# mLSTM cell and mixture of depths on one core: gates of three chunks at once, a first step in its own order, a warm-up of TensorE, and the last batch's picks as matrix products

## Chip, cores, metric

The kernel runs on one core of one Trainium2 chip. The metric is the device time of one execution in microseconds (us).

## The reference

The first part is an mLSTM cell over 4 batches, 8 heads, 768 time steps and head size 40. The second is a mixture of depths: in each batch the 128 tokens with the highest score go through two dense layers (320 to 1024 to 320).

```python
for t in range(S):
    m_new = max(f[t] + m, i[t])
    C = exp(f[t] + m - m_new) * C + exp(i[t] - m_new) * outer(v[t], k[t])
    n = exp(f[t] + m - m_new) * n + exp(i[t] - m_new) * k[t]
    m = m_new
    y[t] = sigmoid(o[t]) * (C @ q[t]) / max(abs(n @ q[t]), 1)
x = y of all heads side by side              # (4, 768, 320)
scores = x @ w_gate
for b in range(4):
    top = the 128 tokens with the highest scores[b]
    out[b] = x[b]
    out[b, top] += sigmoid(scores[b, top]) * (relu(x[b, top] @ w1) @ w2)
```

## The kernel before, in words

The sequence is cut into chunks of 128 tokens, 6 per batch. A step n is one chunk c of one batch b, 24 steps in all. The order of instructions on every engine is that of the program; nothing reorders it.

**A step.** `step(n)` (L466) loads the chunk of step n+4 by four DMAs on SyncE's queue (k, q, v, output gate; `load_chunk`), which come in pieces of 160 bytes. `decay` (POOL, L279) scales the state C. `scores` does the products of keys and queries (PE, pS, L269) and multiplies them by the decay matrix W (DVE, P, L271). W for step n+2 is made in `weigh`: two products (pW, L249), exponential (ACT, L250), and the causal mask (POOL `affine_select`, L251). `scaled_v` makes wv (POOL, L259). `exchange` does the part that comes from the state (pIC, L291 and L297) and updates C. `within` does pH (PE, L319) from P. `norm` makes num, den, rec (DVE) and sor (POOL, L334). `turned(n+2)` turns the keys and queries of step n+2 (PE, pt, L229; ACT copies into T). `result` makes x (DVE, L339), stores it by SyncE, and makes the score sc (DVE, L342). One step later `spread` (PE pb, ACT) and `compare` (DVE ge, L355) count for each token how many score higher.

**The gates.** `gates(c0, c1)` (L162) does the prefix sums of one or two chunks on 32 partitions (4 batches by 8 heads), in three scans and an elementwise chain, and splits both results into three bfloat16 parts each. It is called in the prologue for chunks 0 and 1, and at the end of steps 0 and 2 for chunks 2, 3 and 4, 5. In batch 0, `first_weighed(n+2)` (L458) follows at the end of the step: `operands` (PE pO, ACT a_o, DVE M_o, L197), `weigh`, `scales` (ACT wk and r, L183), `columns` (PE pc, L206, DVE cols) and wv. From step 6 on, W and wv of step n+2 are made in the middle of step n, since the operands of all chunks exist; `operands(1, c)` for batches 2 and 3 are made in steps 4 to 9.

**The second stage.** For batch b-1 it is spread over the steps of batch b: in c=1 `columns_of`, `ranks` and the selection (sel, DVE, L375), in c=2 `gather` (token numbers pidx, then an indirect DMA xe by POOL, L386), in c=3 to 5 the first layer `first` (PE ph, L417, 2, 3 and 3 of 8 blocks f), and in c=0 and c=1 of the batch after it the second layer `second` (PE py, L426, 4 blocks f each), ye and the scatter by POOL (L431). The weights (2.56 MB) are loaded at the end of step 3. After step 23 comes a tail: the last score, comparison and ranks, `second` of batch 2, then for batch 3 the gather from HBM, turning (pX, L398), `first`, `second` and the scatter.

Of the kernel before, what the change touches and what calls it, by code (L numbers as in the profile page):

```python
# [27 lines left out]
def kernel(  # L28
# [123 lines left out]
    nM = gate.tile([BH, NT], FP, name="nM")
    wk = gate.tile([BH, NT, L], FP, name="wk")
    parts = [[gate.tile([BH, NT, L], BF, name=f"{x}{part}") for part in range(3)] for x in "Ma"]
    r = F
# [441 lines left out]
```

## Time and profile before

| | |
|---|---|
| median of 3 runs (lowest to highest) | 258.09 us (255.44 to 258.18) |
| profiled execution: its time, its span | 255.36 us, 253.6 us |
| PE, DVE, POOL, ACT busy | 191.0, 154.7, 104.5, 97.7 us |
| store of x issued, step 0, 5, 6, 12, 18 | 24.8, 94.5, 100.4, 142.6, 186.7 us |

The span is what the trace covers; the time is what is compared. A busy share is a mean over stages with different limits, so the run is read in four stages: until x of step 0, steps 1 to 5 (the rest of batch 0), steps 6 to 23, and the tail. Whenever a "granted clock" is given, 1.00 is 2.4 GHz and 0.50 is 1.2 GHz.

### The profile page before, as it was taken

The numbers are of one execution on the slowest core, as the hardware profiler recorded it, in microseconds if no ns is written. First come the engines' busy times: TensorE is split into PE (matmuls) and PEld (weight loads), VectorE is DVE, ScalarE is ACT, GpSimd is POOL, SyncE is SP. The second block draws the span as 40 slices with busy tenths as digits, with TensorE's granted clock in tenths as the row PEclk, the third lists the DMA queues.
The fourth block names the chain that finished last, engine by engine and source line by source line (L and its number), as shares of the span: only waits on it lengthen the run. The fifth ranks groups of instructions, "written<-read, shape, count | busy, mean of one in ns | idle before, by whom it ended". The sixth has DMA issues, their size and how long they took to land.

```text
span 253.6 us, 6331 instructions
## 1 busy us (share of the span) xinstructions
PE 191.0 (75%) x2522; PEld 160.6 (63%) x2522; DVE 154.7 (61%) x429; ACT 97.7 (39%) x218; POOL 104.5 (41%) x162
## 2 busy tenths in 40 slices
PE   1775366473576988977999999499999988780991
PEld 1464255362464866766999778499987878650880
DVE  7472625158173688889777666977766888740000
ACT  3633521504333565543556536155653641100010
POOL 5235452225316456573345637444563941102001
PEclk9995557575586899998899999889999999997598
DMA  8999900708008999778758987696986100001000
GB/s 111 163 145 145 143 0 16 116 1 125 8 0 270 248 157 145 127 129 141 115 90 127 142 125 98 124 134 103 128 141 83 54 28 27 30 24 52 3 0 27
DMA packets 105454, 24.37 MB, mean 96 GB/s; under 512 B 100496, under 2 KB 104784, under 8 KB 105424
## 3 DMA queue, kind: packets, MB, share of 16 engines
q1 hardware_dynamic: 104896, 22.47, 59.1%
q0 software_dynamic: 384, 1.31, 1.7%
q8 instruction: 20, 0.33, 0.6%
q10 hardware_dynamic: 144, 0.18, 0.3%
q14 instruction: 10, 0.08, 0.1%
HBM read 19.37 MB, written 4.59 MB: 94 GB/s over the span
## 4 chain that ended last, share of the span: by engine, by line
PE 35%; DVE 13%; issue 11%; POOL 5%; DMA 3%; POOLq 1%; ACT 0%; DVEq 0%
PE pH L319 9%; PE pS L269 5%; PE ph L417 5%; PE pt L229 4%; POOL sor L334 4%; PE py L426 3%; DVE x L339 3%; PE pIC L291 3%; DVE scr L342 2%; DVE P L271 2%; DMA out_dram<-ye,idx 2%; PE pIC L297 2%; PE pb L348 2%; DVE num L326 1%; PE pW L249 1%
## 5 line engine op out<-in xcount | busy, mean ns | idle before, releaser
L251 POOL TENSOR_SCALAR_AFFINE_SELECT W<-W 128x512 f32<-128x512 f32 x48 | 31.0, 669 | 54.4 <-ACT W L250 54.4
L334 POOL TENSOR_TENSOR sor<-so,rec 128x320 f32<-128x320 f32 x24 | 24.1, 1005 | 45.9 <-DVE rec L332 42.9
L319 PE MATMUL pH<-v,P 128*64 128x64 f32 x768 | 31.1, 235 | 12.2 <-DVE P L271 12.2
L229 PE MATMUL pt<-ident,qk 128*128 128x128 f32 x192 | 31.1, 314 | 11.7 <-POOL qk L105 6.4
L271 DVE TENSOR_TENSOR P<-pS,W 128x512 f32<-128x512 f32 x48 | 30.8, 682 | 10.4 <-PE pS L269 10.4
L319 PEld LDWEIGHTS pH<-v,P 128*64 128x64 f32 x768 | 27.6, 147 | 14.2 <-DVE P L271 13.4
L250 ACT ACTIVATE W<-pW 128x512 f32<-128x512 f32 x48 | 26.1, 595 | 26.8 <-PE pW L249 20.1
L230 ACT COPY T<-pt 128x512 f32<-128x512 f32 x48 | 26.5, 588 | 21.5 <-PE pt L229 21.5
L229 PEld LDWEIGHTS pt<-ident,qk 128*128 128x128 f32 x192 | 25.7, 162 | 12.7 <-POOL qk L105 6.9
L269 PE MATMUL pS<-T 64*128 64x128 f32 x384 | 32.5, 316 | 0.0
L269 PEld LDWEIGHTS pS<-T 64*128 64x128 f32 x384 | 27.4, 216 | 3.9 <-issue 2.1
L349 ACT COPY sb<-pb 128x128 f32<-128x128 f32 x24 | 6.4, 266 | 60.4 <-PE pb L348 60.4
L417 PE MATMUL ph<-xeT,w 128*128 128x128 f32 x192 | 27.0, 303 | 0.6 <-ACT xeT L400 0.6
L417 PEld LDWEIGHTS ph<-xeT,w 128*128 128x128 f32 x192 | 26.3, 221 | 1.0 <-ACT xeT L400 1.0
L339 DVE TENSOR_TENSOR x<-num,sor 128x320 f32<-128x320 f32 x20 | 14.0, 702 | 14.1 <-POOL sor L334 14.1
L426 PE MATMUL py<-w,hT 128*128 128x320 f32 x64 | 18.5, 434 | 0.0
L291 PE MATMUL pIC<-C,T 128*64 128x82 f32 x320 | 18.0, 262 | 0.0
L291 PEld LDWEIGHTS pIC<-C,T 128*64 128x64 f32 x320 | 14.5, 154 | 4.5 <-issue 3.4
L249 PE MATMUL pW<-M_o,a_o 32*128 32x512 bf16 x48 | 10.9, 427 | 8.4 <-DVE M_o L197 8.4
L431 POOL DMA_INDIRECT out_dram<-ye,idx x4 | 4.1, 1025 | 30.5 <-DVE ye L429 17.2
L355 DVE SCALAR_TENSOR_TENSOR ge<-sb,sc,earlier 128x128 bf16<-128x128 f32 (+5 forms) x24 | 15.7, 655 | 0.8 <-ACT sb L349 0.8
L259 POOL TENSOR_TENSOR wv<-v,cols 128x328 f32<-128x328 f32 x20 | 14.9, 743 | 3.1 <-DVE cols L208 2.4
(107 smaller groups left out, 270.9 us busy)
## 6 DMA issues: line engine op xcount, KB each, us to landing
qk<-in_k_dram SPq DMA_DIRECT2D x24, 160.0 KB, 3.4
qk<-in_q_dram SPq DMA_DIRECT2D x24, 160.0 KB, 4.2
v<-in_v_dram SPq DMA_DIRECT2D x24, 160.0 KB, 4.6
so<-in_o_gate_dram SPq DMA_DIRECT2D x24, 160.0 KB, 4.7
out_dram<-x SPq DMA_DIRECT2D x24, 160.0 KB, 1.8
w<-in_moe_w_dram SPq DMA_DIRECT2D x1, 1280.0 KB, 9.3
w<-in_moe_w_dram SPq DMA_DIRECT2D x2, 512.0 KB, 3.9
w<-in_moe_w_dram SPq DMA_DIRECT2D x1, 256.0 KB, 6.2
```

Of the source, the lines that this page charges most:

```text
L229: nc.tensor.transpose(pt[:, p, :], qk[:, j, 2 * p:2 * p + 2, :].rearrange("s a d -> s (a d)"), ident)
L230: nc.scalar.copy(out=T[:, j], in_=pt)
L250: nc.scalar.activation(out=W[:, h0:h0 + 4, :], in_=pW, func=AF.Exp)
L251: nc.gpsimd.affine_select(out=W[:, h0:h0 + 4, :], in_=W[:, h0:h0 + 4, :], compare_op=OP.is_ge, fill=0.0, base=0, pattern=[[0, 4], [1, L]], ...
L269: nc.tensor.matmul(pS[j][:, p, :], T[e, 0, p, :], T[e, 1, p, :], start=True, stop=True)
L271: nc.vector.tensor_tensor(out=P[:, :, j, :], in0=pS[j], op=OP.mult, in1=W.rearrange("p (n a) t -> p n a t", a=2)[:, :, j, :])
L291: nc.tensor.matmul(pI[t, 2 * p * D1:2 * (p + 1) * D1], T[:, 1, p, t], C[:, p].rearrange("e a d -> e (a d)"), start=True, stop=True)
L319: nc.tensor.matmul(pH[t, 2 * p + j, :], P[:, p, j, t], v1[:, 2 * p + j, :], start=True, stop=True)
L334: nc.gpsimd.tensor_tensor(out=sor, in0=so, in1=rec.unsqueeze(2).to_broadcast([128, H, D]), op=OP.mult)
L339: nc.vector.tensor_tensor(out=x.rearrange("p (h d) -> p h d", d=D), in0=num[:, :, 0:D], in1=sor, op=OP.mult)
L417: nc.tensor.matmul(self.ph[:, f % 4, :], w1[:, j, f * 128:(f + 1) * 128], self.xeT[:, j, :], start=(j == 0), stop=(j == NDC - 1))
L426: nc.tensor.matmul(self.py, self.hT[:, f, :], w2[:, f, :], start=(f == 0), stop=(f == NFC - 1))
```

## The change

- Three chunks lie side by side on 96 partitions (`NR`), so all 24 chunk-and-batch gates take two passes g. `scans` does the sums in each chunk from zero; `ends`, `carry` and `carried` bring the level m from chunk to chunk by small products on PE and one scan; `level` applies it; `split` makes the bfloat16 parts. Pass 0 and the operands of chunks 0 to 2 are done in the prologue, pass 1 beside step 0.
- `columns` turns three chunks at once. The gates come by six DMAs of 32 rows for each of f and i, three of them on SyncE ahead of the first chunk.
- The prologue loads five chunks; step 0 is written out by itself. `warm` runs 8 and then 1 products of 512 columns on a tile of ones that nothing reads.
- `step`: `weights(n+2)` in every step, `turned(n+2)` and `gated(n+2)` ahead of `within`; the causal mask and wv of step n+2 behind `norm`; `operands(0, n+3)` in steps 1 and 2, `operands(1, n-3)` in steps 3 to 8.
- `pieces` (new) deals out the second stage: the selection and gather at the end of steps c=1 and c=2, `first` in 3, 4 and 1 blocks and `second` in 3 and 5, with the scatter at the end of c=0. For batch 2 in the last batch: `first` 4 and 4, `second` 2 and 4, and 2 in the tail.
- Weights are loaded in five parts, one in each of steps 3 to 7.
- Tail: x of the last six steps stays in SBUF (six buffers). The picked rows, already turned, are products of x with the selection (float32, made in three parts): 18 products pX in place of the wait for the gather. The gather still runs, for the gate and the residual.

```diff
+    NR = 3 * BH
+    f_sb = [gate.tile([NR, L], FP, name=f"f_sb{g}") for g in range(2)]
...
+    def load_gates(eng, dst, src, g):
+        for c in range(3):
+            t = slice((3 * g + c) * L, (3 * g + c + 1) * L)
+            eng.dma_start(out=dst[g][c * BH:(c + 1) * BH], in_=src[:, :, t].rearrange("b h p -> (b h) p"))
...
+    def warm(n):
+        pw = ps_m.tile([128, 4 * L], FP, name="pw", tag="m")
+        for _ in range(n):
+            nc.tensor.matmul(pw, earlier[:, 0:128], earlier[:, 0:4 * L], start=True, stop=True)
+    def scans(g):
+        nc.vector.tensor_tensor_scan(out=FM[g][:, 0], data0=ones, data1=f_sb[g], initial=0.0, op0=OP.mult, op1=OP.add)
+        nc.vector.tensor_tensor(out=a[g], in0=i_sb[g], in1=FM[g][:, 0], op=OP.subtract)
+        nc.vector.tensor_tensor_scan(out=FM[g][:, 1], data0=ones, data1=a[g], initial=-BIG, op0=OP.mult, op1=OP.max)
+    def ends(g):
+        pe[g] = ps_m.tile([BH, 3, 2], FP, name="pe", tag="m")
+        for c in range(3):
+            nc.tensor.matmul(pe[g][:, c, :], ident[0:NR, c * BH:(c + 1) * BH], FM[g][:, :, L - 1], start=True, stop=True)
+    def carry(g):
+        e = gate.tile([BH, 3, 2], FP, name="e", bufs=2)
+        nc.vector.tensor_copy(out=e, in_=pe[g])
+        nc.vector.tensor_tensor_scan(out=m[:, 3 * g + 1:3 * g + 4], data0=e[:, :, 1], data1=e[:, :, 0],
+                                     initial=m[:, 3 * g:3 * g + 1], op0=OP.max, op1=OP.add)
+    def carried(g):
+        pm = ps_m.tile([NR, 3], FP, name="pm", tag="m")
+        for c in range(3):
+            nc.tensor.matmul(pm[c * BH:(c + 1) * BH], ident[0:BH, 0:BH], m[:, 3 * g:3 * g + 3], start=True, stop=True)
+        return pm
+    def level(g, pm):
+        own = gate.tile([NR, 3], FP, name="own", bufs=2)
+        nc.vector.tensor_tensor_reduce(out=own, in0=pm, in1=third, scale=1.0, scalar=0.0, op0=OP.mult, op1=OP.add,
+                                       accum_out=m_in[g])
+        nc.vector.tensor_scalar(out=FM[g][:, 1], in0=FM[g][:, 1], scalar1=m_in[g], scalar2=None, op0=OP.max)
+        nc.vector.tensor_scalar(out=nM[g], in0=FM[g][:, 1, L - 1:L], scalar1=-1.0, scalar2=None, op0=OP.mult)
+    def split(g, j, step, cast, sub):
+        x, xs = (FM[g][:, 1], a[g])[j], parts[j][g]
+        if step == 0:
+            rest[j] = gate.tile([NR, L], FP, name=f"rest{j}", bufs=2)
+            cast(out=xs[0], in_=x)
+            sub.tensor_tensor(out=rest[j], in0=x, in1=xs[0], op=OP.subtract)
+        else:
+            cast(out=xs[1], in_=rest[j])
+            sub.tensor_tensor(out=xs[2], in0=rest[j], in1=xs[1], op=OP.subtract)
...
+    def columns(g):
+        pc = ps_m.tile([128, 3, NR], FP, name="pc", tag="m")
+        for j, row in enumerate((wk[g], r[g], r[g][:, L - 1:L].to_broadcast([NR, L]))):
+            nc.tensor.transpose(pc[:, j, :], row, ident[0:NR, 0:NR])
+        both = const.tile([128, 3, NR], FP, name=f"cols{g}")
+        nc.vector.tensor_copy(out=both, in_=pc)
+        for c in range(3):
+            cols[3 * g + c] = both[:, :, c * BH:(c + 1) * BH]
...
+    def load_w1(j):
+        d0, w = HW[j]
...
+        return W
+    def causal(W):
+        for h0 in range(0, H, 4):
...
+        x = x_t[b, c] = work.tile([128, DM], FP, name="x", bufs=NT)
...
+    def select(sel, rank, t0, t1):
...
+    def pieces(b, c, when):
+        early = b == B - 1
+        if when == "late" and b > 1 and c == 0:
+            layers[b - 2].second(3, NFC)
+            layers[b - 2].leave()
+        if b == 0:
+            return
+        own = layers.get(b - 1)
+        if when == "rank":
+            if c == 1:
+                rank = ranks(columns_of(state[b - 1][1][2]), state[b - 1][1][3])
+                sel[b - 1] = mod.tile([128, NT, K_], HF, name="sel", bufs=1)
+                select(sel[b - 1], rank, 0, NT)
+            elif c == 2:
+                picked[b - 1] = gather(b - 1, sel[b - 1], token)
+        elif c == 3:
+            layers[b - 1] = own = Layers(b - 1, *picked[b - 1])
+            own.enter()
+            own.gate()
+            own.first(0, 4 if early else 3)
+        elif c == 4:
+            own.first(4 if early else 3, 8 if early else 7)
+            if early:
+                own.second(0, 2)
+        elif c == 5:
+            if early:
+                own.second(2, 6)
+            else:
+                own.first(7, 8)
+                own.second(0, 3)
 
...
-        P = scores(W[n], T[n])
-        if NT <= n + 2 < N:
-            weighed(n + 2)
+        pS = products(T[n])
+        P = weighted(pS, W[n])
+        if n + 2 < N:
+            W[n + 2] = weights(*steps[n + 2])
         num = exchange(b, c, qk, T[n], wv[n])
...
-            compare(pc, *state[pb][1])
         if n + 2 < N:
-            if n + 2 < NB:
-                pad(nc.gpsimd, n + 2)
             turned(n + 2)
             gated(n + 2)
+        pH = within(P, v1)
+        pb, pc = steps[n - 1]
+        spread(pc, *state[pb][1][:2])
+        num, sor = norm(num, pH, so)
+        if n + 2 < N:
+            causal(W[n + 2])
+            stated(n + 2)
+        compare(pc, *state[pb][1])
         result(b, c, num, sor, state[b][0])
...
+        pieces(b, c, "rank")
+        pieces(b, c, "late")
+        if n + 3 < NT:
+            operands(0, n + 3)
+        if 3 <= n < 3 + NT:
+            operands(1, n - 3)
...
+    load(1)
     nc.sync.dma_start(out=wg, in_=_bcast(moe_w_gate, 128))
-    gates(0, 1)
+    load(2)
+    load(3)
+    load(4)
+    for n in range(1, NB):
+        pad(nc.gpsimd, n)
+    warm(8)
+    scans(0)
+    ends(0)
+    split(0, 1, 0, nc.vector.tensor_copy, nc.vector)
+    carry(0)
...
+    pm = carried(0)
+    split(0, 1, 1, nc.vector.tensor_copy, nc.vector)
+    level(0, pm)
+    for half in range(2):
+        split(0, 0, half, nc.vector.tensor_copy, nc.vector)
...
+    scales(0)
+    operands(0, 1)
     turn(loaded[0][0], 1, T[0])
-    W[0] = weigh(0, 0)
-    scales(0)
+    W[0] = weights(0, 0)
+    columns(0)
+    operands(0, 2)
...
+    scans(1)
+    P = weighted(pS, W[0])
+    W[1] = weights(0, 1)
...
+    turned(1)
+    causal(W[1])
+    stated(1)
+    ends(1)
+    carry(1)
+    pH = within(P, loaded[0][1])
+    pm = carried(1)
+    level(1, pm)
+    W[2] = weights(0, 2)
...
+    result(0, 0, num, sor, state[0][0])
+    scales(1)
+    gated(1)
+    turned(2)
+    operands(0, 3)
+    columns(1)
+    gated(2)
...
-        if n == 0:
-            earlier = const.tile([128, NT * L], BF, name="earlier")
-            nc.gpsimd.memset(earlier, 1.0)
...
+        if 3 <= n < 3 + NDC:
+            load_w1(n - 3)
+        elif 3 + NDC <= n < 5 + NDC:
+            load_w2(n - 3 - NDC)
...
+    spread(u, sc, sb)
+    compare(u, sc, sb, ge, cnt)
+    own.second(6, NFC)
+    rank = ranks(columns_of(ge), cnt)
...
+        nc.gpsimd.memset(last.xeT[w:, NDC - 1], 0.0)
+    pX = ps_m.tile([128, NDC, K_], FP, name="pX", tag="m")
+    for t in range(0, NT, 2):
+        select(sel, rank, t, t + 2)
+    for j, (d0, w) in enumerate(HW):
+        for t in range(NT):
+            nc.tensor.matmul(pX[0:w, j, :], x_t[b, t][:, d0:d0 + w], sel[:, t], start=(t == 0), stop=(t == NT - 1))
+    nc.scalar.copy(out=last.xeT[:, 0:NDC - 1], in_=pX[:, 0:NDC - 1])
+    nc.scalar.copy(out=last.xeT[0:w, NDC - 1], in_=pX[0:w, NDC - 1])
+    own.leave()
+    last.idx, last.xe = gather(b, sel, token_f)
+    last.first(0, NFC)
     last.gate()
-    last.first(0, NFC)
     last.second(0, NFC)
+    last.leave()
```

On GpSimd, steps 13 and 14 (batch 2, c=1 and c=2) stood like this before; C is the decay, W the mask:

```order
L334 TENSOR_TENSOR sor<-so,rec 128x320
L431 DMA out_dram<-ye,idx 768x320
L279 TENSOR_TENSOR C_111<-C_113,cols_432 128x328
L251 AFFINE_SELECT W<-W 128x512 x2
L259 TENSOR_TENSOR wv<-v_107,cols_693 128x328
L386 DMA xe_832<-out_dram,idx 128x320
L334 TENSOR_TENSOR sor<-so,rec 128x320
L279 TENSOR_TENSOR C_112<-C_111,cols_556 128x328
L251 AFFINE_SELECT W<-W 128x512 x2
```

and stand like this now:

```order
L325 TENSOR_TENSOR C_125<-C_124,cols_306 128x328
L380 TENSOR_TENSOR sor<-so,rec 128x320
L295 AFFINE_SELECT W<-W 128x512 x2
L302 TENSOR_TENSOR wv<-v_118,cols_473 128x328
L325 TENSOR_TENSOR C_123<-C_125,cols_306 128x328
L380 TENSOR_TENSOR sor<-so,rec 128x320
L295 AFFINE_SELECT W<-W 128x512 x2
L302 TENSOR_TENSOR wv<-v_119,cols_473 128x328
L433 DMA xe_832<-out_dram,idx 128x320
L325 TENSOR_TENSOR C_124<-C_123,cols_473 128x328
L380 TENSOR_TENSOR sor<-so,rec 128x320
```

The mask and wv moved from ahead of sor to right behind it, the gather from ahead of sor to the end of the step, and the scatter left this stretch (it is now in step 12).

On TensorE, step 16 (batch 2, c=4) before, from its pS to that of the next step:

```order
L269 MATMUL pS<-T 128x128 x8
L249 LDWEIGHTS a_o_943
L249 MATMUL pW<-M_o_942,a_o_943 128x512
L249 LDWEIGHTS a_o_943
L249 MATMUL pW<-M_o_942,a_o_943 128x512
L291 MATMUL pIC<-C_112,T 64x82 x8
L297 MATMUL pIC<-wv,qk_102 64x41 x8
L319 MATMUL pH<-v_107,P 64x64 x16
L348 MATMUL pb<-ident,sc 128x128
L229 MATMUL pt<-ident,qk_104 128x128 x8
L417 MATMUL ph<-xeT,w_164 128x128 x9
L269 MATMUL pS<-T 128x128 x8
```

and now:

```order
L311 MATMUL pS<-T 128x128 x8
L289 LDWEIGHTS a_o_814
L289 MATMUL pW<-M_o_813,a_o_814 128x512
L289 LDWEIGHTS a_o_814
L289 MATMUL pW<-M_o_813,a_o_814 128x512
L337 MATMUL pIC<-C_124,T 64x82 x8
L343 MATMUL pIC<-wv,qk_114 64x41 x8
L269 MATMUL pt<-ident,qk_116 128x128 x8
L365 MATMUL pH<-v_119,P 64x64 x16
L394 MATMUL pb<-ident,sc 128x128
L467 MATMUL ph<-xeT,w_179 128x128 x12
L311 MATMUL pS<-T 128x128 x8
```

The turning pt moved from behind pH to ahead of it, so that it stands where PE waits for P; the first layer now has 12 products (4 blocks) in this step, 9 before.

On TensorE, the end of the program before:

```order
L382 LDWEIGHTS sel
L382 MATMUL pidx<-token,sel 128x1
L398 MATMUL pX<-ident,xe_832 128x128 x3
L417 MATMUL ph<-xeT,w_164 128x128 x24
L426 MATMUL py<-w_165,hT 128x320 x8
```

and now:

```order
L410 MATMUL pcol<-ones_b,ge 128x1
L684 MATMUL pX<-sel,x 128x128 x12
L684 MATMUL pX<-sel,x 64x128 x6
L429 MATMUL pidx<-token_f,sel 128x1 x6
L467 MATMUL ph<-xeT,w_179 128x128 x24
L476 MATMUL py<-w_180,hT 128x320 x8
```

The three transposes of gathered rows became 18 products that read x and sel from SBUF; the index products pidx moved behind them, ahead of the first layer.

## Rows read from the trace of the kernel before

**Rows 1.** Stretches: busy us (count) per engine, granted clock, DMA share, GB/s.

```profile
10.00:20.00 10.00, 6.52 (x52) 5.26 (x51) 5.47 (x14) 5.40 (x14) 4.58 (x10) 0.99 1.52 144
...
30.00:40.00 10.00, 7.10 (x78) 5.85 (x79) 3.47 (x8) 2.02 (x6) 3.63 (x6) 0.50 0.13 13
...
100.00:110.00 10.00, 7.79 (x160) 6.45 (x156) 8.97 (x24) 5.16 (x12) 6.09 (x9) 1.00 0.73 134
...
230.00:240.00 10.00, 5.21 (x23) 4.84 (x24) 0.81 (x4) 0.58 (x2) 1.03 (x1) 0.58 0.07 18
```

**Rows 2.** SyncE queue: start us, us; the stores of x.

```profile
24.82 0.61 SPq L340 DMA_DIRECT2D out_dram<-x  x1
...
88.46 0.95 SPq L340 DMA_DIRECT2D out_dram<-x  x1
...
94.52 0.56 SPq L340 DMA_DIRECT2D out_dram<-x  x1
...
149.31 0.36 SPq L340 DMA_DIRECT2D out_dram<-x  x1
...
160.53 0.36 SPq L340 DMA_DIRECT2D out_dram<-x  x1
```

**Rows 3.** Timeline, steps 1 to 2: start us, us, engine, operation [idle <-releaser].

```profile
46.31 0.75 DVE L197 SCALAR_TENSOR_TENSOR M_o<-pO,of,which 128x512 bf16<-128x512 f32 x1 [2.53 <-ACT a_o L196]
...
48.76 0.38 ACT L183 ACTIVATE wk<-a,nM 32x128 f32<-32x128 f32 x1
...
49.84 2.08 PE L269 MATMUL pS<-T 64*128 64x128 f32 x16
```

**Rows 4.** Timeline, all engines, in the prologue.

```profile
14.75 1.90 PE L229 MATMUL pt<-ident,qk 128*128 128x128 f32 x8
...
15.45 1.27 DVE L271 TENSOR_TENSOR P<-pS,W 128x512 f32<-128x512 f32 x2
```

**Rows 5.** The chain that ended last, step 5: start us, us, what.

```profile
90.16 1.31 PE pH L319 x32
...
92.71 1.26 POOL sor L334
...
95.03 0.66 DVE M_o L197
```

**Rows 6.** The same chain in steps 10 to 12, PE.

```profile
123.63 1.09 PE pS L269 x16
...
125.05 0.72 PE pIC L291 x16
125.77 0.45 PE pIC L297 x16
...
128.29 2.01 PE ph L417 x18
...
140.87 2.15 PE py L426 x8
```

**Rows 7.** Timeline of VectorE in step 14.

```profile
158.92 1.59 DVE L339 TENSOR_TENSOR x<-num,sor 128x320 f32<-128x320 f32 x1 [2.10 <-POOL sor L334]
160.54 0.80 DVE L342 CUSTOM_DVE_ANT_0 scr<-x,wg 128x320 f32<-128x320 f32 x1
```

**Rows 8.** Timeline of GpSimd beside it.

```profile
158.84 0.74 POOL L279 TENSOR_TENSOR C<-C,cols 128x328 f32<-128x328 f32 x1
159.52 1.47 POOL L251 TENSOR_SCALAR_AFFINE_SELECT W<-W 128x512 f32<-128x512 f32 x2
```

**Rows 9.** Timeline of the tail, all engines.

```profile
221.07 0.49 DVE L342 CUSTOM_DVE_ANT_0 scr<-x,wg 128x320 f32<-128x320 f32 x1
...
224.91 0.96 DVE L375 TENSOR_TENSOR sel<-iota_f,rank 128x768 f16<-128x768 f32 x1
...
235.66 8.51 PE L417 MATMUL ph<-xeT,w 128*128 128x128 f32 x48 [0.57 <-ACT xeT L400]
...
244.01 4.47 PE L426 MATMUL py<-w,hT 128*128 128x320 f32 x16
```

More of the change, by code (lines that the diff above doesn't have):

```diff
@@ L146 @@
                                 in_=ident.rearrange("p (g x) -> p g x", x=32)[:, :, 12 * j:12 * j + 12])
-    F = gate.tile([BH, NT, L], FP, name="F")
-    a = gate.tile([BH, NT, L], FP, name="a")
-    Mg = gate.tile([BH, NT, L], FP, name="Mg")
+    FM = [gate.tile([NR, 2, L], FP, name=f"FM{g}") for g in range(2)]
+    a = [gate.tile([NR, L], FP, name=f"a{g}") for g in range(2)]
+    m_in = [gate.tile([NR, 1], FP, name=f"m_in{g}") for g in range(2)]
+    nM = [gate.tile([NR, 1], FP, name=f"nM{g}") for g in range(2)]
@@ L151 @@
+    wk = [gate.tile([NR, L], FP, name=f"wk{g}") for g in range(2)]
+    r = [gate.tile([NR, L], FP, name=f"r{g}") for g in range(2)]
     m = gate.tile([BH, NT + 1], FP, name="m")
[L152 to L155, printed above, removed]
+    parts = [[[gate.tile([NR, L], BF, name=f"{x}{part}{g}") for part in range(3)] for g in range(2)] for x in "Ma"]
@@ L261, in scaled_v, with products @@
         return wv
-    def scores(W, T):
-        P = work.tile([128, NP, 2, L], FP, name="P", bufs=2)
+    def products(T):
         pS = [ps_s.tile([128, NP, L], FP, name="pS") for _ in range(2)]
@@ L447 @@
     loaded, T, W, wv, state = {}, {}, {}, {}, {}
-    layers, sel, picked = {}, {}, {}
+    layers, sel, picked, x_t = {}, {}, {}, {}
     def load(n):
@@ L485, in step @@
-        if b > 0 and c == 1:
-            pcol = columns_of(state[b - 1][1][2])
-        if b > 0 and c == 2:
-            picked[b - 1] = gather(b - 1, sel[b - 1])
-        if b > 0 and c == 3:
-            layers[b - 1] = Layers(b - 1, *picked[b - 1])
-        num, sor = norm(num, pH, so)
-        if n > 0:
-            compare(pc, *state[pb][1])
         if n + 2 < N:
-            if n + 2 < NB:
-                pad(nc.gpsimd, n + 2)
             turned(n + 2)
             gated(n + 2)
-        result(b, c, num, sor, state[b][0])
@@ L501, in step @@
-        if b > 1 and c < 2:
-            layers[b - 2].second(c * NFC // 2, (c + 1) * NFC // 2)
-        if b > 0:
-            if c == 1:
-                sel[b - 1] = ranks(pcol, state[b - 1][1][3])
-            elif c == 3:
-                layers[b - 1].gate()
-                layers[b - 1].first(0, 2)
-            elif c > 3:
-                layers[b - 1].first(3 * c - 10, 3 * c - 7)
-        if n + 2 < NT:
-            if n % 2 == 0:
-                gates(n + 2, n + 4)
-            first_weighed(n + 2)
```

196 lines of the change are left out of this document (83 added, 113 removed).

## The prediction

> **What bounds the kernel now.** I read the stretches first, then the stores of x, then one step of each stage in the timeline or the chain that ended last. The reader should see four stages with four different limits.
>
> *Stage A, until x of step 0:* 24.8 us [rows 2]. VectorE does the gates of chunk 1 ahead of P of step 0, which starts at 15.45 us. TensorE works slowly: eight transposes take 1.90 us [rows 4]. The record calls the clock 0.99 there [rows 1], but 1.90 us is what half clock takes, so the first level in the record is not to be trusted.
>
> *Stage B, steps 1 to 5:* 94.5 - 24.8 = 69.7 us for five steps [rows 2], 13.9 us each. No engine is full: between 30 and 40 us TensorE is busy 7.1 of 10 us, at granted clock 0.50, and VectorE 3.5 [rows 1]. The step is one serial chain: M_o of chunk 3 at 46.31, wk at 48.76, pS of step 2 only at 49.84, since it stands behind them in PE's order, and at half clock pS takes 2.08 us [rows 3] against 1.09 later [rows 6].
>
> *Stage C, steps 6 to 23:* 221.1 - 94.5 = 126.6 us [rows 2, 9], 7.0 us a step. Two kinds of step alternate. Without layer work VectorE's chain sets the pace: pH 1.31, num, den, rec, sor 1.26, x, scr, M_o 0.66, P [rows 5], 6.06 us from store to store [rows 2]. With layer work TensorE is full: from the start of pS to the start of ph 4.66 us, then 2.01 us for three blocks of the first layer [rows 6]. Step 14 takes 11.2 us [rows 2], with the indirect DMAs ahead of sor on GpSimd.
>
> *Stage D, the tail:* from 221.1 to the end of the span at 253.6, 32.5 us. Between sel at 224.91 and the first layer at 235.66 lies the gather through HBM, and the layer then takes 8.51 us [rows 9], because the clock has fallen (0.58 from 230 to 240) [rows 1].
>
> **The change, part by part.** The sum is made against the span of 253.6 us; 1.8 us lie around it, and the profiled 255.4 us are 1% below the median of the runs.
>
> *A.* The scans now serve 96 partitions; their length per partition stays 128, so I cost one at what it was. New in front of M_o of chunk 0 are two small hops over PE and back (ends, carried), which the extra splits cover in part: by my estimate M_o comes 1.5 us later. Behind it VectorE now does two more M_o (0.75 each [rows 3]), one wider copy of columns and pass 1 of the scans (some 1.2 us) ahead of P: P near 15.2, against 15.45 [rows 4], where pass 1 of the gates was already ahead of it. What follows depends on the clock: the warm-up products fill PE until about 5 us, the hops after them leave it idle again. I take x of step 0 at 23.5 us (21 if the clock stays high, 25.5 if not): -1.3. The gate DMAs cost three issues ahead of the first chunk, hidden because pt waits for the splits in PE's order anyway.
>
> *B.* The chain of rows 3 leaves the steps. Operands are made one step earlier than used, one M_o per step stays, and pS needs nothing of it. What is late next is VectorE's chain with M_o: 6.06 us [rows 2], on which I put 0.6 (next paragraph). Step 1 carries the rest of pass 1 on top (two splits with casts on ScalarE, operands, columns ahead of pS): I take 8.5 us. So 8.5 + 4 x 6.66 = 35.1 instead of 69.7: -34.6. Bounds: 5 x 6.06 = 30.3 below; above, half clock all the way (first rival). The constants that GpSimd makes in steps 1 and 3 (some 2 us each) stand behind the mask and wv, not needed before two steps later; uncovered they cost up to 2 us.
>
> *The mask behind sor.* Before, the mask ran while VectorE multiplied P. Now it starts the moment sor ends, when VectorE starts x and then scr. Step 14 shows such a meeting: with decay and mask beside them on GpSimd, x took 1.59 and scr 0.80 us [rows 7, 8] against 0.49 for scr alone [rows 9]. If x alone takes 0.5 like scr, that is 2.39 - 1.0 = 1.4 us, the upper end; zero is the lower, if x wins each time; a gain is excluded, since beside P the mask delayed nothing in this chain. I take 0.6 in each step that VectorE's chain paces, because only one mask pass of 0.6 (1.22 for two undisturbed; here 1.47 [rows 8]) stands ahead of x. The Trainium skill speaks against the move: SBUF — State Buffer, section SBUF: two separate sides, says that a VectorE instruction with two SBUF inputs and a GpSimd instruction that reads SBUF exclude each other for the whole instruction. The trace agrees, by x at 1.59 us. By that rule alone x and scr would each lose a mask pass, 1.2 us.
>
> *C.* With pt ahead of pH, PE fills its wait for P, so a step is paced by PE's sum wherever the layer work is large: 4.66 plus 0.67 per block of the first layer (2.01 / 3) and 0.54 per block of the second (2.15 / 4) [rows 6]. The steps c=0 to c=5 are then: 4.66 - 0.72 + 5 x 0.54 = 6.65 (c=0 has no product with the state, 0.72 [rows 6]); 7.2 (VectorE: 6.06 - 0.66 + 0.6, and 1.2 for rank and sel); 6.0; 4.66 + 0.35 + 2.0 = 7.0 (0.35 for turning the gathered rows: three transposes, of which eight took 1.90 at half clock [rows 4]); 4.66 + 2.7 = 7.35; 4.66 - 0.45 + 0.67 + 1.6 = 6.5 (c=5 makes no new state, 0.45 [rows 6]). That is 40.7 for batch 2. Batch 1 has M_o in its first three steps and no second layer in c=0: 6.66, 7.9, 6.66 for these, 42.1 in all. Batch 3 has more layer work, but no pt and pW (1.2) in its last two steps: 7.65, 7.2 and 5.5 for the last three, 40.2 in all. Sum 123.0 against 126.6: -3.6. The gather stands behind wv now and the scatter one step earlier, so the 11.2 us of step 14 go; that is inside the sum. Total PE work does not shrink, which is why so little comes back. Bounds: 117 with no meeting on the port, 127 with nothing gained.
>
> *D.* Until rank the tail is as before, 3.4 to 3.8 us. The first third of sel comes 0.4 us later, then 18 products pX. They have the shape of those of the first layer, of which 9 take 2.01 us at full clock [rows 6], so 4.0 us. Copies and pidx: 1.3. First layer: 24 products at full clock, 5.4 instead of 8.51. Second layer: 4.3, like 4.47 [rows 9]. From the end of py (244.01 + 4.47 = 248.5) to the end of the span it was 5.1 us and stays. Sum 3.6 + 0.4 + 4.0 + 1.3 + 5.4 + 4.3 + 5.1 = 24.1, with 0.1 of waits 24.2: -8.3. The gather itself (two indirect DMAs in turn on POOL) lies beside first and second layer, 9.7 us; uncovered it would cost what it overruns. If the clock falls, up to twice the 13.7 us of products: +13.7.
>
> Sum: 23.5 + 35.1 + 123.0 + 24.2 = 205.8; with the 1.8 us, 207.6. I predict 208 us.
>
> **The rivals.**
> - *The clock stays low in batch 0 and falls in the tail.* For it: 0.50 at 71% busy [rows 1], and the warm-up ends long before the steps begin; this is also the case that the warm-up does not do what it says. Against it: from 100 us on 1.00 at 78% [rows 1], and the new steps have that density. Price: PE's 4.66 a step doubles to 9.3, with the operands about 10, so four steps of batch 0 lose 4 x 3.4 = 14; the tail alone loses up to 14. About 220.
> - *The port costs twice.* By rows 7 x and scr lose 1.4 instead of 0.6, in 11 steps: 0.8 x 11 = 9, so 216. Against it: the decay, half of that meeting, now comes later. By the rule of the page named above the loss would be 1.2 a step and the time 214.
> - *Loads become the bound.* 640 KB per chunk at 144 GB/s [rows 1] are 4.5 us, under a step of 6.7. In steps 3 to 7 come 0.5 MB of weights and 160 KB of x each: up to 9.2 us at that rate, 5 x 2.5 = 12 too much, of which the load being ahead by two steps takes most. About 213.
> - *More is gained.* No loss on the port, batch 0 at 5.9 us a step, x of step 0 at 21: about 198.
> - *Slower than before.* TensorE is held at 1.2 GHz in the denser program altogether. PE's work at full clock is about 4.7 x 24 = 113 us, 3 x 9.7 = 29 for three batches of layers (8 x 0.67 + 8 x 0.54 each) and 13.7 in the tail, 156 in all; at half clock 312. It decides from the point where the low level costs 48 us, so where 48 of those 156 us are done at it. Against it: 1.00 at 78% [rows 1].
>
> **How the numbers follow.** Forecast 0.52 (203 to 212), low clock 0.13, port 0.11, loads 0.09, more gained 0.12, slower 0.02, and 0.01 that the parts cancel to within the 1% that a measurement of this kernel can tell. Faster by over 1%: 0.97; within 1%: 0.01; slower: 0.02. The range takes in the cheaper case and most of the port and load cases: 198 to 219.
>
> **What would show it.** Store of x of step 0 near 23.5, of step 5 near 59, of step 23 near 182. Right, if pS of a step in batch 0 starts without waiting for wk or M_o, and the clock there is above 0.9. Right for the port, if x has a mean near 1.0 us. Right for the tail, if pX takes 4 us and ph 5.4. Wrong, if stage B exceeds 45 us, if steps 6 to 23 fall below 115 us (then VectorE was not the pace), or if the gate g ends the tail.

## The result, and the profile after

The changed kernel takes 246.4 us (median of 4 runs, 244.6 to 246.7), the kernel before took 257.2 us on the same chip. The ratio is 0.957, 95% interval 0.950 to 0.965: faster, as forecast, but by 11 us and not by 50. The table sets the profiled execution's stages beside the forecast's; they are read as before, from the store of x of step 0 and step 5, and the start of scr of step 23. Executions of one kernel differ by up to 7.1 us; the ratios leave out those over 1.5% above the kernel's fastest, but the stages of mask_and_gather and gather_and_operands, below, come from such a slow execution.

| stage | before | forecast | after |
|---|---|---|---|
| A, until x of step 0 | 24.8 | 23.5 | 24.7 |
| B, steps 1 to 5 | 69.7 | 35.1 | 47.4 |
| C, steps 6 to 23 | 126.6 | 123.0 | 144.8 |
| D, tail | 32.5 | 24.2 | 27.7 |
| span | 253.6 | 205.8 | 244.6 |

B gave two thirds of what was forecast, and C took 18.2 us of it back. SyncE's stores of x, in the timeline of the changed kernel (they answer to [rows 2]; start, us, queue, line, operation):

```profile
24.69 0.41 SPq L386 DMA_DIRECT2D out_dram<-x  x1
72.12 0.36 SPq L386 DMA_DIRECT2D out_dram<-x  x1
149.74 0.36 SPq L386 DMA_DIRECT2D out_dram<-x  x1
160.82 0.36 SPq L386 DMA_DIRECT2D out_dram<-x  x1
```

The third and the fourth are steps 15 and 16: 11.1 us for one step, about as long as step 14 was before. The windows of 10 us of the same kernel (length, then busy us and instructions of PE, PEld, DVE, ACT and POOL, then the granted clock, DMA share, GB/s) answer to [rows 1]:

```profile
20.00:30.00 10.00, 9.32 (x91) 7.27 (x89) 4.95 (x16) 6.13 (x15) 4.00 (x6) 0.50 1.11 156
90.00:100.00 10.00, 9.79 (x113) 8.40 (x113) 6.94 (x19) 3.58 (x8) 5.19 (x6) 0.52 1.27 209
120.00:130.00 10.00, 9.86 (x145) 7.80 (x145) 7.89 (x20) 5.11 (x11) 6.26 (x8) 1.00 0.94 149
140.00:150.00 10.00, 7.32 (x90) 5.92 (x86) 7.02 (x19) 3.27 (x8) 7.21 (x9) 0.75 0.58 101
220.00:230.00 10.00, 8.86 (x49) 8.44 (x50) 1.88 (x6) 0.53 (x2) 1.06 (x2) 0.66 0.06 18
```

The clock falls again in the middle of the run and in the tail. A full TensorE column is therefore no sign of health: 9.79 of 10 us busy for 113 products at 0.52, against 145 products in 9.86 us from 120 to 130 at 1.00.

Three waits are new. The first is in step 2 (timeline, start, us, engine, line, operation; in brackets the idle time before it and what ended it):

```profile
34.28 1.16 PE L311 MATMUL pS<-T 64*128 64x128 f32 x16
...
34.99 0.72 POOL L380 TENSOR_TENSOR sor<-so,rec 128x320 f32<-128x320 f32 x1 [8.25 <-DVE rec L378]
...
35.66 1.47 POOL L295 TENSOR_SCALAR_AFFINE_SELECT W<-W 128x512 f32<-128x512 f32 x2
35.74 0.90 DVE L385 TENSOR_TENSOR x<-num,sor 128x320 f32<-128x320 f32 x1 [0.68 <-POOL sor L380]
36.68 0.80 DVE L388 CUSTOM_DVE_ANT_0 scr<-x,wg 128x320 f32<-128x320 f32 x1
37.11 0.97 POOL L302 TENSOR_TENSOR wv<-v,cols 128x328 f32<-128x328 f32 x1
...
37.41 0.74 DVE L232 SCALAR_TENSOR_TENSOR M_o<-pO,of,which 128x512 bf16<-128x512 f32 x1
...
38.20 0.39 PE L289 MATMUL pW<-M_o,a_o 32*128 32x512 bf16 x2 [2.76 <-DVE M_o L232]
```

pW stands right behind pS and needs the M_o that VectorE makes last of all in step 1; behind pW wait pIC, pt and pH. The same rows show the second: x at 0.90 us and scr at 0.80, against 0.49 undisturbed, with the mask beside them. The third is in steps 14 and 15, the gather of the picked rows:

```profile
141.79 0.80 DVE L388 CUSTOM_DVE_ANT_0 scr<-x,wg 128x320 f32<-128x320 f32 x1
142.22 0.97 POOL L302 TENSOR_TENSOR wv<-v,cols 128x328 f32<-128x328 f32 x1
...
142.52 0.15 DVE L431 TENSOR_SCALAR idx<-pidx 128x1 uint32<-128x1 f32 x1
...
143.35 1.07 POOL L433 DMA_INDIRECT xe<-out_dram,idx  x1 [0.15 <-DVE P L317]
...
149.40 0.55 PE L449 MATMUL pX<-ident,xe 128*128 128x128 f32 x3 [2.62 <-DMA xe<-out_dram,idx]
...
196.79 0.90 PE L449 MATMUL pX<-ident,xe 128*128 128x128 f32 x3 [2.81 <-DMA xe<-out_dram,idx]
...
198.26 5.24 PE L467 MATMUL ph<-xeT,w 128*128 128x128 f32 x24 [0.57 <-ACT xeT L451]
```

pidx was done at 139.1, but idx stands behind x and scr on VectorE, and the indirect DMA behind mask and wv on GpSimd. The rows land 6 us after the issue, and TensorE waits. In the batch after (last two rows) the clock is low behind that wait, and four blocks take 5.24 us, where other kernels below take 2.94. In the kernel before, the same gather had 6.4 us between its issue and pX, and pX did not wait (two lines of its timeline):

```profile
157.05 1.07 POOL L386 DMA_INDIRECT xe<-out_dram,idx  x1 [1.58 <-DVE ge L355]
...
163.49 0.85 PE L398 MATMUL pX<-ident,xe 128*128 128x128 f32 x3
```

### The profile page after: what moved, and what is told of

Read it like the earlier page. It is cut to its first block, busy times and chain, and to the rows that moved or that the text cites. A ratio compares the mean times of both kernels' runs of the same rounds, so it can differ in the third digit from the quotient of the medians.

```text
span 244.6 us, 6426 instructions
## 1 busy us (share of the span) xinstructions
PE 207.7 (85%) x2582; PEld 170.4 (70%) x2582; DVE 158.3 (65%) x414; ACT 93.2 (38%) x207; POOL 107.5 (44%) x157
## 4 chain that ended last, share of the span: by engine, by line
PE 48%; issue 19%; DVE 11%; POOL 10%; DMA 7%; ACT 2%; POOLq 1%; SPq 0%; DVEq 0%
PE pH L365 9%; PE ph L467 8%; PE pS L311 8%; PE pt L269 8%; DMA xe<-out_dram,idx 5%; PE py L476 4%; PE pIC L337 4%; POOL W L295 3%; POOL sor L380 3%; PE pW L289 2%; PE pIC L343 2%; POOL wv L302 2%; DVE x L385 2%; PE pO L227 2%; DVE P L317 2%
## 5 line engine op out<-in xcount | busy, mean ns | idle before, releaser
L380 POOL TENSOR_TENSOR sor<-so,rec 128x320 f32<-128x320 f32 x24 | 24.3, 1014 | 102.4 <-DVE rec L378 102.4
L365 PE MATMUL pH<-v,P 128*64 128x64 f32 x768 | 32.7, 246 | 11.6 <-DVE P L317 11.5
L365 PEld LDWEIGHTS pH<-v,P 128*64 128x64 f32 x768 | 28.8, 156 | 16.7 <-DVE P L317 13.4
L295 POOL TENSOR_SCALAR_AFFINE_SELECT W<-W 128x512 f32<-128x512 f32 x48 | 34.0, 731 | 0.0
L269 PE MATMUL pt<-ident,qk 128*128 128x128 f32 x192 | 33.1, 326 | 1.1 <-ACT W L290 0.7
L467 PE MATMUL ph<-xeT,w 128*128 128x128 f32 x192 | 25.6, 294 | 2.1 <-ACT xeT L451 1.7
L467 PEld LDWEIGHTS ph<-xeT,w 128*128 128x128 f32 x192 | 24.7, 209 | 3.0 <-ACT xeT L451 2.6
L385 DVE TENSOR_TENSOR x<-num,sor 128x320 f32<-128x320 f32 x20 | 17.2, 858 | 12.3 <-POOL sor L380 12.3
L302 POOL TENSOR_TENSOR wv<-v,cols 128x328 f32<-128x328 f32 x20 | 19.1, 953 | 7.3 <-DVE cols L243 7.3
L372 DVE TENSOR_TENSOR num<-num,pH 128x328 f32<-128x328 f32 x20 | 9.9, 496 | 17.9 <-PE pH L365 17.7
L388 DVE CUSTOM_DVE_ANT_0 scr<-x,wg 128x320 f32<-128x320 f32 x24 | 18.8, 783 | 0.8
```

The costliest lines, as they stand in the source:

```text
L269: nc.tensor.transpose(pt[:, p, :], qk[:, j, 2 * p:2 * p + 2, :].rearrange("s a d -> s (a d)"), ident)
L295: nc.gpsimd.affine_select(out=W[:, h0:h0 + 4, :], in_=W[:, h0:h0 + 4, :], compare_op=OP.is_ge, fill=0.0, base=0, pattern=[[0, 4], [1, L]], ...
L302: nc.gpsimd.tensor_tensor(out=wv, in0=v1[:, :, 0:D1], op=OP.mult, in1=cols[c][:, 0, b * H:(b + 1) * H].unsqueeze(2).to_broadcast([128, H, ...
L365: nc.tensor.matmul(pH[t, 2 * p + j, :], P[:, p, j, t], v1[:, 2 * p + j, :], start=True, stop=True)
L380: nc.gpsimd.tensor_tensor(out=sor, in0=so, in1=rec.unsqueeze(2).to_broadcast([128, H, D]), op=OP.mult)
L467: nc.tensor.matmul(self.ph[:, f % 4, :], w1[:, j, f * 128:(f + 1) * 128], self.xeT[:, j, :], start=(j == 0), stop=(j == NDC - 1))
```

## The experiments

All runs start from the changed kernel. The table has each kernel's median (lowest to highest), its ratio to the kernel before on the same chip with its 95% interval where there is one, and the stages of its profiled execution.

| kernel | us | ratio | A | B | C | D |
|---|---|---|---|---|---|---|
| the change | 246.4 (244.6-246.7) | 0.957 (0.950-0.965) | 24.7 | 47.4 | 144.8 | 27.7 |
| mask_back | 232.6 (230.4-233.8) | 0.904 (0.896-0.912) | 24.7 | 44.9 | 137.7 | 24.7 |
| gather_early | 233.4 (232.2-233.8) | 0.913 (0.908-0.917) | 24.3 | 48.4 | 133.1 | 24.7 |
| operands_early | 239.7 (239.3-240.8) | 0.936 (0.930-0.942) | 24.3 | 42.1 | 146.4 | 24.7 |
| turn_back | 253.8 (250.3-257.0) | - | 24.7 | 47.9 | 152.7 | 24.7 |
| filler | 254.7 (253.4-255.7) | 0.993 (0.990-0.996) | 24.7 | 50.5 | 153.7 | 24.9 |
| no_warm | 243.5 (239.9-245.4) | 0.954 (0.947-0.961) | 24.5 | 45.3 | 143.6 | 24.7 |
| mask_and_gather | 229.9 (227.4-232.1) | 0.888 (0.879-0.897) | 24.6 | 44.4 | 133.0 | 27.5 |
| gather_and_operands | 230.8 (225.2-231.9) | - | 24.6 | 44.0 | 133.4 | 27.6 |
| three_moves | 222.5 (220.8-224.4) | 0.872 (0.866-0.878) | 24.7 | 39.9 | 129.7 | 24.7 |
| three_no_warm | 222.9 (220.0-225.0) | 0.875 (0.871-0.879) | 24.5 | 39.5 | 129.6 | 24.7 |
| three_long_warm | 222.6 (220.3-227.5) | 0.865 (0.861-0.869) | 24.6 | 39.5 | 131.5 | 26.2 |
| layers_in_gap | 224.6 (222.4-226.7) | 0.876 (0.871-0.880) | 24.6 | 39.4 | 133.4 | 24.7 |

**The mask (mask_back).**

```diff
+        if n + 2 < N:
+            causal(W[n + 2])
+            stated(n + 2)
         num, sor = norm(num, pH, so)
-        if n + 2 < N:
-            causal(W[n + 2])
-            stated(n + 2)
```

> The mask and wv of step n+2 go back ahead of sor on GpSimd; nothing else moves. Theory port: x falls from a mean of 0.86 to about 0.5 us and scr from 0.78 to 0.5, so some 0.65 us a step come back on VectorE's chain; in the 10 to 20 steps that this chain paces that is 6 to 13 us, 233 to 240. Rival (TensorE's waits and its clock pace steps 6 to 23, VectorE has slack): x and scr fall alike, the time stays at 244 to 247.

Measured: 232.6 us. The groups by line (busy us, mean ns, idle before them), first of the change, then of this kernel:

```profile
L295 POOL TENSOR_SCALAR_AFFINE_SELECT W<-W 128x512 f32<-128x512 f32 x48 | 34.0, 731 | 0.0
L388 DVE CUSTOM_DVE_ANT_0 scr<-x,wg 128x320 f32<-128x320 f32 x24 | 18.8, 783 | 0.8
L385 DVE TENSOR_TENSOR x<-num,sor 128x320 f32<-128x320 f32 x20 | 17.2, 858 | 12.3 <-POOL sor L380 12.3
```

```profile
L295 POOL TENSOR_SCALAR_AFFINE_SELECT W<-W 128x512 f32<-128x512 f32 x48 | 31.2, 674 | 27.2 <-ACT W L290 27.1
L385 DVE TENSOR_TENSOR x<-num,sor 128x320 f32<-128x320 f32 x20 | 13.4, 672 | 12.3 <-POOL sor L380 12.3
L388 DVE CUSTOM_DVE_ANT_0 scr<-x,wg 128x320 f32<-128x320 f32 x24 | 12.7, 531 | 0.8
```

x and scr lose 3.8 and 6.1 us of busy time; the rival, that VectorE has slack, falls. Not all of the 13.8 us gained is the mask's. The profiled execution is 2.5 us shorter in B, 7.1 in C and 3.0 in D, and in D nothing was moved: the same 36 products pX ran at half clock in the change and at full clock here.

```profile
220.79 7.29 PE L684 MATMUL pX<-sel,x 128*128 128x128 f32 x36 [0.80 <-DVE sel L423]
```

```profile
211.11 4.37 PE L684 MATMUL pX<-sel,x 128*128 128x128 f32 x36 [0.80 <-DVE sel L423]
```

x did not come down to 0.5 as expected: in seven steps it still takes 1.01 us, beside the decay on GpSimd.

**The turning (turn_back).**

```diff
-        if n + 2 < N:
-            turned(n + 2)
-            gated(n + 2)
         pH = within(P, v1)
+        if n + 2 < N:
+            turned(n + 2)
+            gated(n + 2)
```

> The turning of the chunk of step n+2 (pt, its copies, the tanh) goes back behind pH; nothing else moves. Theory gap: TensorE's one long wait for P (2.1 to 2.8 us) is split in two shorter ones, the clock stays at 1.00 in steps 6 to 23 and the products that follow take 1.09 (pS) instead of 2.08: 238 to 242. Rival order: pt (0.72 us) stands between pH and the next pS again and is no longer hidden by the wait for P, the clock falls as before: 248 to 258.

Measured: 253.8 us, as the rival said. The waits of TensorE for P (total, count, longest), first of the change, then of this kernel:

```profile
PE pH L365 <- DVE P L317: 11.5, 6, 2.6
```

```profile
PE pH L365 <- DVE P L317: 17.3, 8, 3.3
```

The granted clock in C is 0.90 here and 0.91 in the change. The place ahead of pH is a gain, of some 4 to 11 us by the executions (250.3 to 257.0), and not the cause of the loss; the theory that TensorE's one long wait should be split falls.

**The operands (operands_early).**

```diff
+        if n + 3 < NT:
+            operands(0, n + 3)
+        if 3 <= n < 3 + NT:
+            operands(1, n - 3)
         pH = within(P, v1)
...
         pieces(b, c, "late")
-        if n + 3 < NT:
-            operands(0, n + 3)
-        if 3 <= n < 3 + NT:
-            operands(1, n - 3)
```

> The operands of a later chunk (pO, a_o, M_o) are made ahead of pH in the step instead of at its end; nothing else moves. Theory order: pW of steps 2 and 3 no longer waits 2.8 us for M_o, and M_o of steps 1 to 8 lies in VectorE's wait for pH instead of on its chain: steps 1 to 5 take 40 to 43 us instead of 47.4, and 1 to 2 us come back in steps 6 to 8: 238 to 242. Rival clock: the stage is slow because TensorE runs at half clock from 10 to 30 us, the waits only move to another product: 244 to 247.

Measured: 239.7 us, B 42.1. Timeline of step 2:

```profile
32.57 0.75 DVE L232 SCALAR_TENSOR_TENSOR M_o<-pO,of,which 128x512 bf16<-128x512 f32 x1 [2.11 <-ACT a_o L231]
33.53 0.39 PE L289 MATMUL pW<-M_o,a_o 32*128 32x512 bf16 x2
```

pW has no wait here, and M_o lies in an idle time of VectorE. The theory stands for B, with 5.3 us; C gained nothing (146.4 against 144.8). That the time lies in the theory's range is in part luck: 3.0 of the 6.7 us are the clock of the tail, as with mask_back.

**Filling the waits (filler).**

```diff
+    def fill(tile, n):
+        for _ in range(n):
+            nc.tensor.matmul(tile, earlier[:, 0:128], earlier[:, 0:4 * L], start=True, stop=True)
-    def within(P, v1):
+    def within(P, v1, n=0):
         pH = ps_h.tile([128, H, DP], FP, name="pH")
+        fill(pH.rearrange("t h d -> t (h d)"), n)
...
-        pH = within(P, v1)
+        pH = within(P, v1, 4)
...
+    fill(ps_h.tile([128, H, DP], FP, name="pH").rearrange("t h d -> t (h d)"), 6)
     for t in range(0, NT, 2):
```

> Four products of 512 columns on the tile of ones stand ahead of pH in each of steps 1 to 23, and six ahead of pX in the tail; their results are overwritten or unread. Theory gap: the wait for P and the wait for sel are what lets the clock fall; filled, the clock reads 1.00 from step 3 on, no pS takes 2 us, pX takes 4.0 us instead of 7.3: 230 to 240 (each filler of 0.9 us lies in a wait of 2.1 us). Rival: the clock is low for another reason; the fillers take 1.7 us at half clock and delay pH in the steps with layer work: 250 to 265.

Measured: 254.7 us. The clock did for the most part what the theory said: 1.00 in the windows from 60 to 100 us, and from 120 to 150, but 0.67 from 100 to 110. The time did what the rival said, for another reason. Step 11 of this kernel, at full clock:

```profile
118.26 1.16 PE L311 MATMUL pS<-T 64*128 64x128 f32 x16
119.49 1.28 DVE L317 TENSOR_TENSOR P<-pS,W 128x512 f32<-128x512 f32 x2
...
121.46 1.03 PE L362 MATMUL pH<-earlier 128*128 128x512 bf16 x4
122.41 1.15 PE L370 MATMUL pH<-v,P 128*64 128x64 f32 x32
```

P is ready at 120.8, before the filler starts: in this step there is no wait to fill, and four products cost their 1.03 us. Seven steps (11 to 13, 17 to 19 and 23) are 0.86 us longer each than in the change, 6 us in all. Steps 9 and 10 take another 3.5 us more, where pX now waits 3.04 us for the rows asked for in step 8, and itself takes 0.87 us. Here, buying the clock with idle work cost more than it gave.

**The gather (gather_early).**

```diff
         num, sor = norm(num, pH, so)
+        pieces(b, c, "rank")
...
-        pieces(b, c, "rank")
```

> Ranks and selection in c=1, token numbers and the gather xe in c=2 go ahead of x on VectorE and of mask and wv on GpSimd (behind sor); nothing else moves. Theory gather: xe is asked for about 2.8 us sooner, the wait of 2.6 to 2.8 us ahead of pX in three steps goes, and with it the half clock that follows it there: 9 to 14 us less than the change, 233 to 238. Rival: the wait was slack, the next step's chain on VectorE ends as late as before and x of c=1 and c=2 is 1 us later: 244 to 248.

Measured: 233.4 us, C 133.1 against 144.8. The group of pX in c=3 (busy us, mean ns, idle before it), first of the change, then of this kernel:

```profile
L449 PE MATMUL pX<-ident,xe 128*128 128x128 f32 x9 | 1.9, 334 | 5.4 <-DMA xe<-out_dram,idx 5.4
```

```profile
L449 PE MATMUL pX<-ident,xe 128*128 128x128 f32 x9 | 1.6, 285 | 1.8 <-DMA xe<-out_dram,idx 1.8
```

Of the 11.7 us, 3.6 are the wait itself. Most of the rest is TensorE's work at a higher clock: in C its 1781 instructions are busy for 119.4 us instead of 127.0, at a mean granted clock of 0.97 instead of 0.91. Step 16, the long one, takes 8.2 us instead of 11.1. It takes 11.1 to 14.1 us in all six kernels without this move, and 7.7 to 9.3 in six of the seven with it (12.3 in layers_in_gap).

**The warm-up (no_warm, three_no_warm, three_long_warm).** The first two leave out both lines with `warm`, the second and third stand on the three moves.

```diff
-    warm(1)
+    warm(4)
...
     turn(loaded[0][0], 0, T[0])
+    warm(3)
     operands(0, 0)
```

> The nine products on the tile of ones in the prologue are left out; nothing reads their result. Theory: the clock is back at half by 9.65 us whatever stands before, so only pt of chunk 0 (0.66 us, then 1.1) is slower and x of step 0 comes at 25.1 instead of 24.7; the time stays at 246 to 247. Rival (the warm-up pays): half clock from the start costs 2 us or more by step 0, 248 to 250.

> The three moves without the nine warm-up products. Theory: they bring nothing, 221 to 223.5. Rival (they pay): 225 or more.

> The three moves with three more warm-up products ahead of the turning of chunk 0 and three behind its first half, which fill TensorE's waits between 5.8 and 8.6 us. Theory (short waits there let the clock fall at 9.65 us): the products from 10 to 30 us run at full clock, x of step 0 at 21 to 22, step 1 about 3 us shorter: 216 to 218. Rival (the clock falls there for another reason, or VectorE's hops pace the prologue): 221 to 224.

Measured: A is 24.5 without and 24.7 with the warm-up. The change without it takes 243.5 us (239.9 to 245.4), less than theory or rival expected. In its profiled execution the clock came back sooner (pS of step 1 takes 1.16 us at 24.50 and not 2.08 us at 25.97), B is 2.1 us shorter, and the tail again 3.0. On the three moves the times are 222.9 without and 222.5 with it. It pays nothing. The longer one (222.6 us, as its rival said) gives full clock to the second half of chunk 0's turning (0.66 us for four at 9.33 instead of 1.11), but pS of step 0 takes 2.08 us again at 12.61, though TensorE had waited only 0.55 and 0.52 us in between. Why the clock falls there stays open.

**Together (three_moves, and two of them at a time).** The three edits above in one kernel, and the gather's with each of the others.

> Mask and wv ahead of sor, ranks and gather right behind sor, and operands ahead of pH, together. Theory that the three causes are separate: stage B 40, steps 6 to 23 some 12 us under the 145 of the change by the port and some 10 us by the gather, the tail at 26: 218 to 226. Rival (the same waits are counted twice, another chain takes over after the first): 228 to 233, no better than the move of the mask alone.

> The moves of mask and wv and of ranks and gather, without that of the operands. Theory (the meeting of mask with x and scr costs time of its own, beside what the mask delays the gather): with the gather already early, the mask's move still takes 4 to 8 us off steps 1 to 23, 226 to 229. Rival (the mask's move helped only because it let the gather start sooner): 232 to 234, as the move of the gather alone.

> The moves of ranks and gather and of the operands, without that of the mask. Theory: the operands' move is worth 5 to 6 us in steps 1 to 5 whatever else is moved, 227 to 229, with x and scr still at 0.80 and 0.76. Rival (stage B is paced by the clock or by the port once M_o is out of the way): 231 to 234.

Measured: 222.5, 229.9 and 230.8 us. Alone the moves are worth 13.8 (mask), 12.9 (gather) and 6.7 (operands), 33.4 in sum; together 23.8. The stages show where the difference lies. The tail takes 27.7 us in the change's profiled execution and 24.7 in those of the three single moves and of three_moves, though its code is the same. So 3.0 us of it are counted in each single worth, and only once in the joint one: 6.0 of the 9.6 us. In B and C together the moves bring 9.6, 10.7 and 3.7 us, 24.0 in sum, and 22.6 when made at once. Outside the tail the three causes are nearly separate, as the theory said.

What a move adds to the others is less certain, since the executions of the two pairs lie far apart (227.4 to 232.1, 225.2 to 231.9). By the medians the mask as the last of the three adds 8.2 us and the operands 7.4, by each kernel's fastest execution 4.4 and 6.6. All executions of three_moves (220.8 to 224.4) are below those of both pairs, so each of the two is worth something as the last. The first pair also lies below gather_early (232.2 to 233.8), so the rival that the mask's move only let the gather start sooner falls; for the second the runs do not decide. Mask and operands without the gather were not run.

TensorE's busy time, first of the change, then of three_moves (first part of the page):

```profile
PE 207.7 (85%) x2582; PEld 170.4 (70%) x2582; DVE 158.3 (65%) x414; ACT 93.2 (38%) x207; POOL 107.5 (44%) x157
```

```profile
PE 192.6 (88%) x2582; PEld 156.2 (71%) x2582; DVE 147.6 (67%) x414; ACT 92.0 (42%) x207; POOL 104.7 (48%) x157
```

As many instructions, 2582, are busy for 15.1 us less, at a mean granted clock of 0.92 instead of 0.85; 2.9 us of it are pX in the tail.

**Second-layer blocks in the wait (layers_in_gap).** On top of the three moves:

```diff
         if when == "late" and b > 1 and c == 0:
-            layers[b - 2].second(3, NFC)
-            layers[b - 2].leave()
+            layers[b - 2].second(2, 5)
+        if when == "gap":
+            if b > 1 and c == 1:
+                layers[b - 2].second(5, NFC)
+            return
+        if when == "late" and b > 1 and c == 1:
+            layers[b - 2].leave()
...
-                own.second(0, 3)
+                own.second(0, 2)
...
+        pieces(b, c, "gap")
         pH = within(P, v1)
```

> The three moves, and in each of the batches 2 and 3 the last three blocks of the second layer of two batches before stand in TensorE's wait ahead of pH of c=1 (1.6 us there) instead of one in c=5 and two in c=0; ye and the scatter follow at the end of c=1. Theory (TensorE's sum paces c=5 and c=0, VectorE's chain paces c=1): 1.6 us a batch go, 3 us in all, 219 to 220.5. Rival (these steps wait for VectorE anyway, or pH of c=1 is delayed by as much): 222 to 223.

Measured: 224.6 us, above both expectations: no gain. In step 13 (c=1 of batch 2) the three blocks delay pH, for which VectorE waits:

```profile
115.89 1.78 PE L476 MATMUL py<-w,hT 128*128 128x320 f32 x6
117.61 1.15 PE L365 MATMUL pH<-v,P 128*64 128x64 f32 x32
118.81 0.50 DVE L372 TENSOR_TENSOR num<-num,pH 128x328 f32<-128x328 f32 x1 [2.66 <-PE pH L365]
```

pt had ended at 116.06. Against three_moves, c=0 and c=1 are still 0.5 and 0.4 us shorter in each of the two batches, but c=2 is 1.2 us longer, and step 16 takes 12.3 us instead of 9.3. There ph, behind a wait of pX of 1.76 us, ran at half clock: its first 18 instructions took 4.21 us, where in three_moves they took 2.27 behind a wait of 1.53. three_moves and its versions with another warm-up are the fastest found, 0.865 to 0.875 of the kernel before with times that overlap, where the change has 0.957.

## Why the prediction was wrong, step by step

- **Direction:** right. **A:** 24.7 against 23.5. "The clock stays high" or not was named as what decides; it falls by 9.65 us and stays at 0.50 until pt of step 1 is done at 32.6 us, so the rival that the warm-up does not do what it says was true here.
- **B** came to 47.4, over the 45 us that the forecast named as a sign of being wrong. It failed on "Operands are made one step earlier than used, one M_o per step stays, and pS needs nothing of it". The text looked at pS alone, and pS indeed does not wait. operands(0, n+3) stands at the end of step n, and its user is not step n+3 but pW in step n+1, ahead of everything else on TensorE. Step 1 took 12.0 us (forecast 8.5), steps 2 and 3 took 9.8 and 9.95 (6.66 each). Making the operands earlier gave 5.3 us in B; with all three moves B is 39.9. Step 1 is not mended by any of them: it takes 10.7 to 12.6 us in all runs, two thirds of it at the low clock in the change.
- **C, the gather,** failed on "The gather stands behind wv now ... so the 11.2 us of step 14 go". Step 14 fell from 11.2 us [rows 2] to 8.2, but two steps later, in step 16, stands one of 11.1 us. Before, the indirect DMA was issued in the middle of step 14, its rows landed in 3.1 us, and pX did not wait. Now it is issued behind step 14, at 143.35, among the loads of a chunk (k, q, v and gate, issued from 142.23 to 144.09), and the rows take 6.0 us; the forecast took "0.35 for turning the gathered rows" and never asked when they land. Moved early, C is 133.1.
- **C, the port:** the size was right and the reach was not. x and scr lose 0.41 and 0.31 us in a step where they meet the mask, 0.72 against the 0.6 I took. By the Trainium skill's rule alone (SBUF — State Buffer, section SBUF: two separate sides) it would have been at most 1.2, a whole pass for each. The trace agrees with the exclusion: x takes 0.90 us instead of 0.49 in 18 of the 24 steps. That each operation loses only the rest of the pass that it meets would fit the smaller loss, and is not shown. But I counted the loss in some 11 steps, on the sum "4.66 plus 0.67 per block", which takes TensorE's products at full clock and VectorE's chain as hidden in the other steps. C is 21.8 us over the forecast, and the port's own loss is 13 us at most (0.72 in 18 steps). In places longer waits for P were followed by products at half clock, as in step 14, where pS takes 2.08 us:

```profile
137.20 1.38 PE L365 MATMUL pH<-v,P 128*64 128x64 f32 x32 [2.23 <-DVE P L317]
...
139.05 2.08 PE L311 MATMUL pS<-T 64*128 64x128 f32 x16
```

- **The low clock** was a rival (0.13) for batch 0 and the tail only. It fell in batches 1 to 3, where the forecast held 1.00 at 78% busy [rows 1] for safe: 0.52 from 90 to 100 us, 0.75 from 140 to 150. Over C it is 0.91, and 0.96 where the filler fills waits; that waits bring the clock down fits both, but not every wait did: the products behind the wait of 2.62 us at 149.40 ran at full clock, those behind 2.81 us at 196.79 at half.
- **The loads** as bound (0.09) did not come: the list of waits of the change has none for a chunk's k, q, v or gate after the prologue, only for the gathered rows (5.4 us of TensorE in two steps, 3.3 of VectorE in the tail).
- **D:** 27.7 against 24.2. The terms were right: ph took 5.60 (5.4), py 4.47 (4.3), and the gather lay beside them. pX took 7.29 instead of 4.0, at half clock. In nine other profiled executions the same 36 products took 4.3 or 4.4 us and the tail 24.7 to 24.9, in two 7.3 and in one 5.9. So the term was right at full clock. Which clock it meets is not settled by the tail's own code, which is the same; each kernel was profiled once, so whether it goes with the kernel or with the execution stays open.
- **What is left:** three_moves has a span of 219.0 against the forecast's 205.8. B is 4.8 over, 4.1 of it in step 1 (12.6 against 8.5), and C 6.7. Of C, batch 2 takes 44.4 us against 40.7 (stores of steps 11 and 17): rank and sel now stand ahead of x in c=1, which takes 9.4 us against 7.2, and c=4, behind the gather, takes 9.3 against 7.35.

## What to carry to other kernels

When instructions change places, follow each one to its consumer on the other engines and write down when its result is needed in the order there: the forecast did this for the wait that went (pS) and not for the next in the queue (pW, pX). Ask of a transfer when it lands, not only what it stands behind. A wait on TensorE costs its own length and may cost the low clock behind it; take the wait away by order, since filling it with idle products cost 8 us here. And before the worths of single changes are added up, look by stage whether each holds the same piece, here the 3.0 us of the tail.
